# Unused tiles between the operand tiles of TensorE: the places of a fused attention and MoE kernel's tiles in SBUF

## The chip, the core and the metric

The kernel runs on one core of a Trainium2 chip, as one program. The metric is the time of one execution on the device in microseconds, given as the median of three runs. Beside the timed runs there is one profiled execution, and every duration below is read from it.

## What is computed

The first half is a linear attention with a decaying state (4 batches, 8 heads, 768 steps, 48 elements a head); the second half is a dense layer pair with a gate, on 3072 rows of 384:

```python
for t in range(S):
    cur = einsum('bhd,bhe->bhde', u[None] * kt, vt)
    y[:, :, t] = einsum('bhd,bhde->bhe', rt, state + cur)
    state = w[None, :, :, None] * state + einsum('bhd,bhe->bhde', kt, vt)
...
x = y.transpose(0, 2, 1, 3).reshape(B * S, H * D)
h = x @ w_in                # 3072x384 by 384x2048
g = h * cos(h)
out = g @ w_out             # 3072x2048 by 2048x384
```

The MoE weights come in double precision, read as pairs of 32-bit words.

## The kernel before

**The dense part.** Each number of x, w_in, w_out and g is held as a high part and a low part, both of the type fp32r, so that one product takes three matmuls: high by high, high by low, low by high. The rows of x stand in chunks of 128, and three chunks make a block of 384 columns; there are eight blocks. For each block and each of 16 slices of 128 columns of w_in, `mm_h` (L350 to L360) issues nine matmuls: the stationary operand is a 128x128 piece of `w_in_hi` or `w_in_lo`, the moving one is 128x384 of `xh` or `xl` (three runs of 512 bytes in each partition). Its order for one of three parts of the sum is xh with w_in_hi, xl with w_in_hi, xh with w_in_lo. ScalarE and VectorE then turn the result in PSUM into `gh` and `gl` (`whole`, `rest`, `cosine`, and the operations named f_gate, f_gh and f_gl). `mm_o` (L362 to L366) issues three matmuls for each of the three chunks: the stationary operand is a 128x128 piece of gh, gl, gh, and the moving one 128x384 of `w_out_hi`, `w_out_hi`, `w_out_lo`. So there are 8 x 16 x (9 + 9) = 2304 matmuls of 128x384, here called the large ones. Each has a LDWEIGHTS of its own, 128 columns of four bytes, that is 512 bytes in each partition.

**The attention part** is cut into 24 chunks, which TensorE works on between the large matmuls: transposes (L819), scores (L911, L1210), state sums (L978, L1216), outputs (L932, L945, L1283), all in plain fp32 with far smaller shapes. The double-precision weights are read and split (`conv`, L731 to L743) in the first half of the run.

**Order.** A planner in the kernel (`Plan`) gives every operation a cost, a buffer of a ring and a due time, and writes out one order for all engines; a table of due times (`DUES`) sets the order of the first part. It knows nothing of addresses.

**Places in SBUF.** Tiles are laid one behind the other in the order in which the code asks for them. The first 16384 bytes of each partition are the scratch in which GpSimd writes the descriptors of its DMAs (here `dma_start(..., accum_op=ALU.add)`, 27 times). The tiles that the large matmuls read have sizes that are multiples of 512 bytes, and an unused tile of 80 words ahead of them (`const.tile([P, 80], F32, name="gap")`) makes the first of them start at a multiple of 512. So all of them do: w_in_hi, w_in_lo, w_out_hi, w_out_lo, xh, xl, and the rings gh0 to gh2 and gl0 to gl2. Every 128x128 piece of a stationary operand starts 512 bytes, or a multiple of that, behind the start of its tile, and so does every run of a moving one. The last tile ends 352 bytes before the end of the partition's 229376.

Of the kernel before, what the change touches and what calls it, by code (L numbers as in the profile page):

```python
# [9 lines left out]
F32 = mybir.dt.float32  # L10
F32R = mybir.dt.float32r
# [278 lines left out]
def kernel(  # L290
# [11 lines left out]
    nc = tc.nc  # L302
# [5 lines left out]
    P = 128  # L308
# [13 lines left out]
    TB = max(BLOCKS) * C  # L322
# [6 lines left out]
    wts = ctx.enter_context(tc.tile_pool(name="wts", bufs=1))  # L329
# [9 lines left out]
    w_in_hi = wts.tile([P, NK, DFF], F32R, name="w_in_hi")  # L339
    w_in_lo = wts.tile([P, NK, DFF], F32R, name="w_in_lo")  # L340
    w_out_hi = wts.tile([P, NF, DM], F32R, name="w_out_hi")
    w_out_lo = wts.tile([P, NF, DM], F32R, name="w_out_lo")

    w_in_w = moe_w_in.bitcast(I32)
# [35 lines left out]
    with ExitStack() as actx:  # L380
        att = actx.enter_context(tc.tile_pool(name="att", bufs=1))
# [10 lines left out]
        def ring(name, n, shape, dtype):  # L392
            return [Tile(att.tile(shape, dtype, name=f"{name}{i}")) for i in range(n)]
# [9 lines left out]
        R_A = [Tile(A_all[:, n]) for n in range(4)]  # L403
        R_ar = [Tile(A_all[:, n : n + 2], R_A[n : n + 2]) for n in (0, 2)]
        xh = att.tile([P, XS, NK, C], F32R, name="xh")
        xl = att.tile([P, XS, NK, C], F32R, name="xl")
        R_x = [Tile((xh[:, i], xl[:, i])) for i in range(XS)]

        R_f = ring("f", 6, [P, DM], F32)
        R_qi = ring("qi", 1, [P, TB], I32)  # L410
        R_gh = ring("gh", 3, [P, TB], F32R)
        R_gl = ring("gl", 3, [P, TB], F32R)
        R_raw = ring("raw", 2, [P, DM, 2], I32)


# [928 lines left out]
        for i in range(2 * NF):  # L1344
            plan.group = 100 + i
            f, part = divmod(i, 2)
# [18 lines left out]
        for s, (n, f, f0, f1) in enumerate(steps):  # L1365
# [4 lines left out]
            ph, q, qi, gh, gl = Buf(B_H if n >= GRP else B_HX), Buf(R_f), Buf(R_qi), Buf(R_gh), Buf(R_gl)  # L1370
# [128 lines left out]
    with tc.If(ok < 1, label="general"):  # L1499
        with ExitStack() as gctx:  # L1500
            cp = gctx.enter_context(tc.tile_pool(name="cp", bufs=1))
            for i in range(2 * NF):
                f, part = divmod(i, 2)
# [131 lines left out]
```

## Time and profile before

| | |
|---|---|
| median of 3 runs | 489.88 us (489.73 to 490.03) |
| the profiled execution | 489.98 us |
| its span, from the first to the last instruction | 488.3 us |
| outside the span | 1.7 us |
| TensorE, matmuls busy | 481.6 us of the span, 99% |
| TensorE, weight loads busy | 465.6 us, 95% |
| VectorE, ScalarE, GpSimd busy | 379.3, 301.6, 221.1 us |
| granted TensorE clock, mean | 0.997 of 2.4 GHz |

The ends of matmuls in the profile are modelled, and successive matmuls overlap: the 334 ns that the page gives for a large one is the time from its start to its modelled end, not the time that it takes from the next. That is read from the distance between the starts of two matmuls that follow each other.

### The profile page before, as it was taken

What the parts mean: (1) busy time and instruction counts of PE and PEld (TensorE: products, weight loads), DVE (VectorE), ACT (ScalarE), POOL (GpSimd) and SP (SyncE); (2) the same over time, 40 slices, a digit from 0 to 9 for tenths busy, and PEclk for the clock granted to TensorE, in tenths of its full rate; (3) what the DMA queues carried; (4) which work ended last, traced back from release to release, by engine and by line L of the source; (5) the groups of instructions that cost most, each with busy time, mean ns of one, the idle gap of its engine ahead of it and who ended that gap; (6) DMA issues with size and microseconds to landing.
All of it is one profiled execution on the core that took longest, in us unless ns stands there. A gap on an engine that the chain in (4) does not pass through costs nothing.

```text
span 488.3 us, 12920 instructions
## 1 busy us (share of the span) xinstructions
PE 481.6 (99%) x4939; PEld 465.6 (95%) x4939; DVE 379.3 (78%) x790; ACT 301.6 (62%) x718; POOL 221.1 (45%) x227
## 2 busy tenths in 40 slices
PE   8999999999999999999999999999999999999995
PEld 7888999999999999999999999999999999999995
DVE  6988898878999677686896886877867967865552
ACT  5999777767777555556456455465564654644452
POOL 7786225544434856546446245545364275200000
PEclk9999999999999999999999999999999999999998
DMA  8885276865667863766645735655456466100001
GB/s 160 166 191 141 67 221 153 186 155 134 160 156 138 140 121 52 173 104 144 138 97 138 154 92 140 134 158 133 98 128 143 129 148 142 34 30 20 2 0 53
DMA packets 130903, 59.47 MB, mean 122 GB/s; under 512 B 107892, under 2 KB 126740, under 8 KB 130836
## 3 DMA queue, kind: packets, MB, share of 16 engines
q1 hardware_dynamic: 126740, 53.04, 44.2%
q0 software_dynamic: 3888, 5.31, 7.9%
q8 instruction: 40, 0.66, 0.6%
q10 hardware_dynamic: 208, 0.25, 0.1%
q14 instruction: 27, 0.22, 0.1%
HBM read 48.55 MB, written 10.03 MB: 120 GB/s over the span
## 4 chain that ended last, share of the span: by engine, by line
PE 97%; ACT 2%; issue 0%; DVE 0%; DVEq 0%; ACTq 0%
PE bank L366 42%; PE bank L360 41%; PE bank L1210 3%; PE bank L1283 3%; PE bank L819 2%; PE bank L911 2%; PE bank L945 2%; ACT A L884 1%; PE bank L1481 1%; PE bank L932 1%; PE bank L978 1%; ACT kT L861 0%; ACT zt L960 0%; PE bank L583 0%; ACT f L1443 0%
## 5 line engine op out<-in xcount | busy, mean ns | idle before, releaser
L366 PE MATMUL bank<-w_out_hi,gh 128*128 128x384 f32 x384 | 130.9, 341 | 0.0
L360 PE MATMUL bank<-xh,w_in_hi 128*128 128x384 f32 x384 | 129.0, 336 | 0.0
L366 PE MATMUL bank<-w_out_lo,gh 128*128 128x384 f32 x384 | 128.5, 335 | 0.0
L366 PE MATMUL bank<-w_out_hi,gl 128*128 128x384 f32 x384 | 128.4, 334 | 0.0
L360 PE MATMUL bank<-xh,w_in_lo 128*128 128x384 f32 x384 | 128.4, 334 | 0.0
L360 PE MATMUL bank<-xl,w_in_hi 128*128 128x384 f32 x384 | 128.3, 334 | 0.0
L371 ACT ACTIVATE qi<-bank 128x384 int32<-128x384 f32 (+1 forms) x132 | 63.1, 481 | 75.3 <-PE bank L360 74.5
L374 DVE SCALAR_TENSOR_TENSOR f<-bank,qi 128x384 f32<-128x384 f32 (+1 forms) x132 | 70.9, 539 | 31.6 <-ACT qi L371 30.7
L377 ACT ACTIVATE f<-f 128x384 f32<-128x384 f32 (+1 forms) x132 | 67.7, 516 | 44.3 <-DVE f L374 41.5
L1404 DVE TENSOR_TENSOR bank<-bank,f 128x384 f32<-128x384 f32 x126 | 70.7, 561 | 29.1 <-ACT f L377 26.3
L1410 DVE TENSOR_TENSOR gl<-bank,gh 128x384 fp32r<-128x384 f32 x126 | 69.4, 550 | 19.4 <-ACT gh L1407 18.7
L1407 ACT CAST gh<-bank 128x384 fp32r<-128x384 f32 x126 | 60.2, 478 | 38.1 <-DVE bank L1404 35.6
L366 PEld LDWEIGHTS bank<-w_out_hi,gh 128*128 128x128 f32 x384 | 72.0, 188 | 1.7
L360 PEld LDWEIGHTS bank<-xh,w_in_hi 128*128 128x128 f32 x384 | 72.1, 188 | 0.6 <-issue 0.2
L360 PEld LDWEIGHTS bank<-xh,w_in_lo 128*128 128x128 f32 x384 | 72.1, 188 | 0.1
L366 PEld LDWEIGHTS bank<-w_out_hi,gl 128*128 128x128 f32 x384 | 72.1, 188 | 0.0
L360 PEld LDWEIGHTS bank<-xl,w_in_hi 128*128 128x128 f32 x384 | 72.1, 188 | 0.0
L366 PEld LDWEIGHTS bank<-w_out_lo,gh 128*128 128x128 f32 x384 | 72.1, 188 | 0.0
L731 POOL TENSOR_TENSOR f<-f,raw 128x384 int32<-128x384 int32 x32 | 35.2, 1101 | 55.5 <-DVE f L722 24.1
L1152 POOL TENSOR_TENSOR kT<-kT,decT_k 112x512 f32<-112x512 f32 x14 | 18.3, 1310 | 80.1 <-DVE kT L1137 75.1
L1157 POOL TENSOR_TENSOR A<-rT,decT_r 48x512 f32<-48x512 f32 x28 | 36.2, 1292 | 20.7 <-DVE rT L1137 19.6
L1191 POOL TENSOR_TENSOR A<-ident,a 64x512 f32<-64x512 f32 x28 | 30.1, 1074 | 19.7 <-DVE a L1183 18.2
(121 smaller groups left out, 627.8 us busy)
## 6 DMA issues: line engine op xcount, KB each, us to landing
raw<-in_moe_w_in_dram SPq DMA_DIRECT2D x32, 384.0 KB, 3.4
raw<-in_moe_w_out_dram SPq DMA_DIRECT2D x32, 384.0 KB, 3.5
out_dram<-f POOLq DMA_DIRECT2D x27, 192.0 KB, 4.5
out_dram<-f SPq DMA_DIRECT2D x23, 192.0 KB, 2.4
raw<-in_k_dram SPq DMA_DIRECT2D x55, 80.0 KB, 3.1
raw<-in_r_dram SPq DMA_DIRECT2D x55, 80.0 KB, 2.3
k<-in_k_dram SPq DMA_DIRECT2D x28, 96.0 KB, 2.8
f<-in_r_dram SPq DMA_DIRECT2D x28, 96.0 KB, 2.9
```

The lines of the kernel that those rows point to most:

```text
L360: nc.tensor.matmul(ph, a, b_, start=(i == 0), stop=(i == len(mm) - 1))
L366: nc.tensor.matmul(acc, a[:, ts], b_[:, f, :], start=(first and i == 0), stop=(last and i == 2))
L371: nc.scalar.activation(qi, ph, AF.Copy, scale=INV_2PI, bias=0.25)
L374: nc.vector.scalar_tensor_tensor(q, ph, INV_2PI, qi, op0=ALU.mult, op1=ALU.subtract)
L377: nc.scalar.activation(q, q, AF.Sin, scale=TWO_PI, bias=0.5 * math.pi)
L731: return lambda: eng.tensor_tensor(ai(), ai(), cn(), op=ALU.add)
L1152: nc.gpsimd.tensor_tensor(d, d, late_d(decT_k)[0:KP], op=ALU.mult)
L1157: nc.gpsimd.tensor_tensor(by_batch(plane(ar, j))[rows[j]], by_batch(late_t(rT))[rows[j]], late_d(decT_r)[rows[j]], op=ALU.mult)
L1191: nc.gpsimd.tensor_tensor(plane(ar, j)[side[j]], ident2[side[j], None, :].to_broadcast(to), ab()[side[j], :, None].to_broadcast(to), op=AL ...
L1404: nc.vector.tensor_tensor(g()[:, cs], ph()[:, cs], q()[:, cs], op=ALU.mult)
L1407: nc.scalar.copy(gh()[:, cs], g()[:, cs])
L1410: nc.vector.tensor_tensor(gl()[:, cs], g()[:, cs], f32(gh())[:, cs], op=ALU.subtract)
```

## The change

Unused tiles are laid between the operand tiles, so that they no longer all start at the same place within 512 bytes, and the scratch for DMA descriptors is halved to make room:

```diff
     w_out_hi = wts.tile([P, NF, DM], F32R, name="w_out_hi")
+    wts.tile([P, 64], F32, name="gap_w")
     w_out_lo = wts.tile([P, NF, DM], F32R, name="w_out_lo")
...
         xh = att.tile([P, XS, NK, C], F32R, name="xh")
+        att.tile([P, 96], F32, name="gap_x")
         xl = att.tile([P, XS, NK, C], F32R, name="xl")
+        att.tile([P, 96], F32, name="gap_f")
...
-        R_gh = ring("gh", 3, [P, TB], F32R)
-        R_gl = ring("gl", 3, [P, TB], F32R)
+        R_gh, R_gl = [], []
+        for ring_g, name, gaps in ((R_gh, "gh", (64, 16, 48)), (R_gl, "gl", (64, 32, 32))):
+            for i, gap in enumerate(gaps):
+                att.tile([P, gap], F32, name=f"gap_{name}{i}")
+                ring_g.append(Tile(att.tile([P, TB], F32R, name=f"{name}{i}")))
+        att.tile([P, 64], F32, name="gap_r")
...
-    nc = _bacc.Bacc("TRN2", target_bir_lowering=False, num_devices=1)
+    nc = _bacc.Bacc("TRN2", target_bir_lowering=False, num_devices=1, dynamic_dma_scratch_size=8192)
```

A word is four bytes, so the starts of the tiles, as the rest after division by 512, become:

| tile | before | after |
|---|---|---|
| w_in_hi, w_in_lo, w_out_hi | 0 | 0 |
| w_out_lo, and the attention's k, v, r, kT, rT and A tiles behind it | 0 | 256 |
| xh | 0 | 256 |
| xl | 0 | 128 |
| f (six buffers), qi | 0 | 0 |
| gh0, gh1, gh2 | 0, 0, 0 | 256, 320, 0 |
| gl0, gl1, gl2 | 0, 0, 0 | 256, 384, 0 |
| raw (two buffers) and the state tiles behind it | 0 | 256 |

The unused tiles are written and read by nothing. The instructions, their order on each of the five engines and the semaphores that they wait for are the same row for row; only the addresses differ, and the line numbers of the file (a line of before stands 1 further down from L342 on, 2 from L406 on, 3 from L407 on and 7 from L413 on).

While a large matmul streams its moving operand, TensorE loads the stationary operand of the next matmul. There are 2276 places in the program where one large matmul directly follows another. Counted over the program's order, the start of the stationary piece that is loaded, less the start of the moving operand that is being read, modulo 512, is:

| stationary less moving, modulo 512 | 0 | 64 | 256 | 320 | 384 |
|---|---|---|---|---|---|
| places before | 2276 | 0 | 0 | 0 | 0 |
| places after | 372 | 122 | 1140 | 129 | 513 |

The 372 are those in which gh2 or gl2 is loaded while w_out_hi is read (252), and those in which gh0 is loaded while w_out_lo or xh is read (120).

## Rows read from the trace of the kernel before

**Rows 1.** The page's first part: busy time, share of the span, instructions.

```profile
PE 481.6 (99%) x4939; PEld 465.6 (95%) x4939; DVE 379.3 (78%) x790; ACT 301.6 (62%) x718; POOL 221.1 (45%) x227
```

**Rows 2.** The chain that ended last, shares of the span by engine and by line.

```profile
PE 97%; ACT 2%; issue 0%; DVE 0%; DVEq 0%; ACTq 0%
PE bank L366 42%; PE bank L360 41%; PE bank L1210 3%; PE bank L1283 3%; PE bank L819 2%; PE bank L911 2%; PE bank L945 2%; ACT A L884 1%; PE bank L1481 1%; PE bank L932 1%; PE bank L978 1%; ACT kT L861 0%; ACT zt L960 0%; PE bank L583 0%; ACT f L1443 0%
```

**Rows 3.** Waits of TensorE: us in total, times, longest us.

```profile
PE bank L1481 <- DVE pq L474: 1.2, 1, 1.2
PE bank L911 <- ACT kT L861: 0.2, 1, 0.2
```

**Rows 4.** Busy time by stretch: length, then busy (instructions) of each engine.

```profile
core 0: us, PE busy (x) PEld busy (x) DVE busy (x) ACT busy (x) POOL busy (x), PEclk, DMA share, GB/s
58.00:168.00 110.00, 110.00 (x635) 109.78 (x634) 95.91 (x203) 79.39 (x179) 51.80 (x53) 1.00 0.68 158
60.00:80.00 20.00, 20.00 (x118) 20.00 (x117) 18.96 (x45) 15.62 (x38) 5.41 (x6) 1.00 0.59 189
120.00:160.00 40.00, 40.00 (x233) 40.00 (x232) 36.05 (x75) 29.17 (x66) 17.95 (x19) 1.00 0.68 150
```

**Rows 5.** Timeline near 130 us: start, length, engine, line.

```profile
129.90 0.33 PE L360 MATMUL bank<-xh,w_in_hi 128*128 128x384 f32 x1
129.90 0.19 PEld L360 LDWEIGHTS bank<-xl,w_in_hi 128*128 128x128 f32 x1
130.07 0.33 PE L360 MATMUL bank<-xl,w_in_hi 128*128 128x384 f32 x1
130.07 0.19 PEld L360 LDWEIGHTS bank<-xh,w_in_lo 128*128 128x128 f32 x1
130.25 0.33 PE L360 MATMUL bank<-xh,w_in_lo 128*128 128x384 f32 x1
130.25 0.19 PEld L360 LDWEIGHTS bank<-xh,w_in_hi 128*128 128x128 f32 x1
```

**Rows 6.** One line's matmuls, L819: duration min/median/max, first and last start.

```profile
L819 PE MATMUL bank<-ident,vr x40: 272/273/421, 5.7 to 38.3; 128*112 128x128 f32 x40
```

**Rows 7.** Timeline of TensorE's matmuls near 38 us: transposes.

```profile
38.02 0.60 PE L819 MATMUL bank<-ident,vr 128*112 128x128 f32 x4
```

**Rows 8.** Groups of weight loads by shape: count, busy us, mean ns of one.

```profile
L366 PEld LDWEIGHTS bank<-w_out_hi,gl 128*128 128x128 f32 x384 | 72.1, 188 | 0.0
...
L1283 PEld LDWEIGHTS bank<-A,vr 128*32 128x32 f32 x448 | 12.9, 109 | 2.2 <-DVE bank L1404 1.0 <-issue 1.0 <-DVE gl L1410 0.2
```

**Rows 9.** Timeline of TensorE's matmuls at 217 us, after a stretch of small ones.

```profile
217.22 0.44 PE L366 MATMUL bank<-w_out_hi,gh 128*128 128x384 f32 x1
217.50 0.33 PE L366 MATMUL bank<-w_out_hi,gl 128*128 128x384 f32 x1
217.66 0.34 PE L366 MATMUL bank<-w_out_lo,gh 128*128 128x384 f32 x1
217.84 0.35 PE L360 MATMUL bank<-xh,w_in_hi 128*128 128x384 f32 x1
218.03 0.34 PE L360 MATMUL bank<-xl,w_in_hi 128*128 128x384 f32 x1
```

**Rows 10.** Timeline of TensorE's matmuls at 170 us, the second and the eighth large one.

```profile
170.36 0.34 PE L366 MATMUL bank<-w_out_hi,gl 128*128 128x384 f32 x1
...
171.43 0.33 PE L360 MATMUL bank<-xl,w_in_hi 128*128 128x384 f32 x1
```

**Rows 11.** Timeline of TensorE's matmuls near 47 us: scores, then large ones.

```profile
47.13 0.39 PE L911 MATMUL bank<-rT,kT 48*128 48x128 f32 x4
```

**Rows 12.** One line's matmuls, L911: duration min/median/max, first and last start.

```profile
L911 PE MATMUL bank<-rT,kT x160: 272/272/373, 8.6 to 47.2; 48*128 48x128 f32 x160
```

**Rows 13.** The page's groups on other engines that touch the moved tiles.

```profile
L1410 DVE TENSOR_TENSOR gl<-bank,gh 128x384 fp32r<-128x384 f32 x126 | 69.4, 550 | 19.4 <-ACT gh L1407 18.7
L1407 ACT CAST gh<-bank 128x384 fp32r<-128x384 f32 x126 | 60.2, 478 | 38.1 <-DVE bank L1404 35.6
L731 POOL TENSOR_TENSOR f<-f,raw 128x384 int32<-128x384 int32 x32 | 35.2, 1101 | 55.5 <-DVE f L722 24.1
```

**Rows 14.** Waits over all engines, the longest of ScalarE for TensorE.

```profile
ACT qi L371 <- PE bank L360: 74.5, 83, 3.1
```

**Rows 15.** GpSimd's DMAs: the line's issues and the time to landing.

```profile
L1455 POOL DMA_DIRECT2D out_dram<-f x27: 862/1012/1522, 80.3 to 209.7; - x27
...
DMA to landing us min/median/max: 3.6/4.5/6.3
```

## Prediction

> **What bounds the kernel now.** I read the busy times first, then the chain of work that ended last, the stretches, and last the starts of single matmuls. TensorE is busy for 481.6 of 488.3 us [rows 1] and holds 97% of the chain, 83 points of it in the two lines of the large matmuls [rows 2]. It waited for other engines for 1.4 us in the whole run [rows 3], so what one large matmul takes from the next is what the kernel takes.
>
> That distance is read from a stretch in which nothing but large matmuls runs, 58 to 168 us: 110 us hold 635 of them, 173.2 ns each [rows 4]. The single starts say the same (129.90, 130.07, 130.25), and show the next weight load starting with each matmul, not after it [rows 5]. The clock granted there is 1.00 of 2.4 GHz [rows 4], at which 384 columns, one a cycle, are 160 ns. What does a stream of matmuls with a load each cost on top? The transposes tell: four of 128 columns span 0.60 us with a last one of 0.272 [rows 6, 7], so they follow each other by (0.60 - 0.272)/3 = 109 ns, which is 2 cycles a column (106.7 ns) and 2.5 ns. By that a large matmul would take 160 + 2.5 = 162.5 ns. It takes 10.8 more. Over the 2276 places where one follows another this is 2276 x 10.8 ns = 24.6 us: the stake of this change, 5% of the run.
>
> Where do the 10.8 ns come from? Loading is not too slow by itself: a load of 128 columns is recorded with 188 ns, one of 32 with 109 [rows 8], so a column is 79/96 = 0.82 ns and 128 columns are 105 ns, well under 173. But the two streams do disturb each other. After a stretch of small matmuls the distances are not 173 at once: at 217 us they run 0.16, 0.18, 0.19 [rows 9], and at 170 us six of them take 171.43 - 170.36 = 1.07 us, 178 ns each [rows 10]. The same instructions on the same kind of tiles take anything from about 168 to 185 ns, until they settle at 173. Only the moment at which the load starts within the matmul differs.
>
> **The change part by part.** No instruction is added, removed or moved, so all of the cost is in durations.
>
> *The distance of the loaded piece from the streamed operand.* At all 2276 places it is 0 modulo 512 before; after, it is something else at 2276 - 372 = 1904. The trace of before holds no large matmul at another distance, so the price is bounded from both sides by the nearest rows. If the 10.8 ns are a collision of the two reads that only equal places bring, all of it goes: 1904 x 10.8 = 20.6 us. If the new distance acts as another phase does, the shortest distance seen (0.16, taken as 168 ns [rows 9]) gives 1904 x 5 = 9.5 us back, and the mean of an unsettled row (178 ns [rows 10]) costs 1904 x 5 = 9.5 us; the longest seen (0.19, about 185 ns) would be 1904 x 12 = 23 us lost. The value I take is 0, for three reasons. First, the tiles before differ in all places above 512 bytes (pieces of w_in, w_out, g and three runs of x at ever new addresses), and 173 holds over all of them in the long stretch [rows 4]: nothing in this trace goes by place. Second, equal places alone do no harm: the scores read kT and rT, both at 0 modulo 512, and four of them span 0.39 us [rows 11] with 0.272 for the last [rows 12], so the second pair starts 0.12 us after the first at most, about the 109 ns of the transposes, whose two operands lie at different places (ident at 160). Both have a column every two cycles. What the large ones have that these have not is a full-rate stream, one column a cycle: a shared rate of reading, which would not care for addresses, fits this as well as a collision. Third, a phase of a nanosecond or two already changes the distance [rows 9, 10], and 64 to 384 bytes are many columns; if the two streams settle by themselves after any disturbance, they may settle at the same 173 from any start.
>
> The Trainium skill speaks against an effect too: its page "TensorE: Matmul & The Clock Gate", section "Step-by-step: what each phase is for", gives TensorE two independent read ports to SBUF, one for the moving operand and one for weight loads, so that loading the next weights takes nothing from the running matmul. By it the change is worth 0. The trace agrees only in part: the same page's section "Back-to-back issue gap" has N/2.4 + 2.5 ns, 162.5 for 384, and the 173.2 ns [rows 4] are not that. So what the page rules out is happening in some form, and no run of before shows in which.
>
> *The writers.* ScalarE writes gh, VectorE reads it and writes gl, GpSimd reads f and raw: 478, 550 and 1101 ns each [rows 13]. All new starts are multiples of 64 bytes and each operation still runs over the same contiguous words, so I take 0. These lie behind TensorE: ScalarE alone waits 74.5 us for it [rows 14]. If each of the 126 gl were 5% slower, that is 3.5 us spread over the run, inside VectorE's idle time of 488 - 379 = 109 us [rows 1]. Without that cover, at the fullest stretch (18.96 of 20 us busy, 60 to 80 us [rows 4]), 5% would be 1 us on the path.
>
> *Half the scratch for GpSimd's descriptors.* It serves 27 DMAs, all issued between 80.3 and 209.7 us, one in 4.8 us on average, each landed within 6.3 us [rows 15]. So about one is open at a time, and a ring of half the size has to hold no more than that. If one waits for room, GpSimd's later work (the sums of `conv`, the decays) waits behind it; GpSimd is busy for 17.95 of 40 us there [rows 4]. I take 0, with at most one landing, 6.3 us, which would have to stand in a place without cover.
>
> *Sum:* 489.98 us of the profiled execution (span 488.3 and 1.7 around it), less 0. The median of the three runs is 489.88, 0.1 below it; I give 489.8.
>
> **The rivals.**
>
> *Equal places collide, and the collision goes.* For it: the 10.8 ns are there, and phase matters. Against it: the scores. It gives 489.98 - 20.6 = 469.4. Part could be lost in new waits: TensorE needs results 6% sooner, and in the fullest stretch VectorE's 18.96 us stand against 20.0 - 1904/2276 x 20.0 x 10.8/173.2 = 18.96. VectorE would just hold there and all later stretches are emptier (36.05 of 40). With 1 us for it, 470.4.
>
> *Another phase, a part of it:* the streams settle nearer to the shortest distance seen: 489.98 - 9.5 = 480.5, and anything between that and no change.
>
> *The other side: the streams settle worse.* Today they lock at 173 after each disturbance; at new distances, of which there are five, changing from matmul to matmul, they may never settle, and keep the 178 ns seen at 170 us [rows 10]. That gives 489.98 + 9.5 = 499.5. It decides against the change as soon as the mean over the 1904 places is above 173.7, since 1904 x 0.5 ns is 1 us.
>
> *The room for descriptors binds:* GpSimd's DMA issues, now 0.86 to 1.52 us long [rows 15], become several us long; at most 6.3 us, 496, and more likely hidden. I count it in the slower cases.
>
> **How the numbers follow.** A measurement of this kernel tells changes from about 0.2%, 1 us, on (three runs lie within 0.3 us). No change: 0.33, the likeliest single case, at 489.8, with 489.0 to 490.7 as its own range. The collision goes: 0.24. A part of it: 0.19. Slower, by unsettled streams (0.21) or by descriptors (0.03): 0.24. So faster 0.24 + 0.19 = 0.43, same 0.33, slower 0.24. Cases of both signs hold most of the chance, so the range reaches to both: from 469, the foot of the full gain, to 499, the unsettled price, which leaves out a gain at more places than the 1904, and streams that run worse than 178 ns, together under 0.2.
>
> **What would show it.** In the stretch 58 to 168 us the count of large matmuls: 635 again if places don't matter; 1904/2276 of 10.8 ns less, 164.3 on average, would put 670 there; 178 would put 618. By kind: if equal places collide, the large matmuls before a load of gh2 or gl2 keep 173 and those before gh1 or gl1 fall to 162.5, within one run; if all three buffers show the same distance, place is not the cause. The groups of the other engines [rows 13] should stay within 2% of 550, 478 and 1101 ns; if gl or gh move by more, the writers were mis-sized. L1455 should keep a median near 1.0 us; several us would show the smaller scratch. The prediction is wrong if the distance of large matmuls is not 173 in that stretch, in either direction, and right for the wrong reason if distances change by kind and cancel.

## The result, and the profile after

The changed kernel takes 493.14 us, median of 3 runs (492.95 to 493.7), against 489.88: ratio 1.0069, 95% interval 1.0046 to 1.0092. It became slower by 3.3 us, where no change was forecast; the time still lies inside the stated range of 469 to 499 us. Its profiled execution also took 493.14 us, with a span of 491.3 us.

The page's first part and the chain that ended last, after:

```profile
PE 484.6 (99%) x4939; PEld 468.8 (95%) x4939; DVE 381.0 (78%) x790; ACT 301.8 (61%) x718; POOL 221.2 (45%) x227
...
PE 97%; ACT 2%; issue 0%; DVE 0%; DVEq 0%; ACTq 0%
```

TensorE is busy for 3.0 us more than in [rows 1] with the same 4939 instructions, and holds the same 97% of the chain as in [rows 2]. Its waits for other engines are those of [rows 3] to the tenth of a microsecond:

```profile
PE bank L1488 <- DVE pq L481: 1.2, 1, 1.2
PE bank L918 <- ACT kT L868: 0.2, 1, 0.2
```

So the time did not go into a new wait. The stretch that [rows 4] begin with, after:

```profile
58.00:168.00 110.00, 110.00 (x631) 110.00 (x631) 95.75 (x202) 79.11 (x179) 50.99 (x52) 1.00 0.67 157
```

Four large matmuls fewer stand in the same 110 us, at the same granted clock of 1.00: 174.3 ns each, where it was 173.2. Which ones became longer is seen in the groups of TensorE's lines (count, busy us, mean ns of one). Two groups after:

```profile
L361 PE MATMUL bank<-xl,w_in_hi 128*128 128x384 f32 x384 | 130.7, 340 | 0.0
...
L361 PE MATMUL bank<-xh,w_in_lo 128*128 128x384 f32 x384 | 128.7, 335 | 0.0
```

and the first of them before:

```profile
L360 PE MATMUL bank<-xl,w_in_hi 128*128 128x384 f32 x384 | 128.3, 334 | 0.0
```

The matmul that reads xl grew by 6 ns, from start to modelled end. While it runs, the piece of w_in_lo for the next matmul is loaded, and this is the largest kind of place whose distance became 384. The one behind it, which reads xh, is at 335.

To price it, I took the starts of all 2304 large matmuls from both traces, and added up by kind what each takes until the next starts, at the 2276 places where one directly follows another:

| what is read, while what is loaded | places | distance after, modulo 512 | mean before, ns | mean after, ns | change in all, us |
|---|---|---|---|---|---|
| xl while w_in_lo | 384 | 384 | 173.4 | 179.0 | +2.15 |
| w_out_hi while gl1 | 129 | 384 | 179.4 | 181.6 | +0.29 |
| w_out_lo while gh1 | 84 | 64 | 174.0 | 176.3 | +0.20 |
| xh while gh1 | 38 | 64 | 173.7 | 172.6 | -0.04 |
| w_out_hi while gh1 | 129 | 320 | 173.7 | 173.3 | -0.05 |
| xh while w_in_hi | 645 | 256 | 174.6 | 175.1 | +0.28 |
| all others | 867 | 0 or 256 | | | +0.21 |

(The means hold the first matmul behind each of the 28 stretches of small ones, 283 ns on average; these fall mostly on the places where gl is loaded. Without them, the places where gl1 is loaded go from 173.4 to 175.8 ns.) The rows add up to 3.03 us. The rest of the span stayed: the first large matmul starts at 39.04 us before and 39.03 after, the stretches of small matmuls between the large ones take 45.44 and 45.40 us in all, and the tail behind the last large start 5.59 and 5.68. So 3.03 of the 3.08 us by which the span grew lie in these distances, and seven tenths of them at the 384 places of xl.

The other engines, after:

```profile
L1417 DVE TENSOR_TENSOR gl<-bank,gh 128x384 fp32r<-128x384 f32 x126 | 69.4, 551 | 19.6 <-ACT gh L1414 19.2
L1414 ACT CAST gh<-bank 128x384 fp32r<-128x384 f32 x126 | 60.3, 478 | 36.7 <-DVE bank L1411 35.7
...
L738 POOL TENSOR_TENSOR f<-f,raw 128x384 int32<-128x384 int32 x32 | 35.2, 1102 | 55.7 <-DVE f L729 22.9
```

They stand at 551, 478 and 1102 ns, within 1 ns of [rows 13]. GpSimd's DMA line, after, is as in [rows 15], with a median landing of 4.9 us for 4.5:

```profile
L1462 POOL DMA_DIRECT2D out_dram<-f x27: 859/1012/1517, 80.5 to 210.8; - x27
```

### The profile page after: what moved, and what is told of

It is laid out like the page before. It is cut to its first block, busy times and chain, and to the rows that moved or that the text cites. A ratio compares the mean times of both kernels' runs of the same rounds, so it can differ in the third digit from the quotient of the medians.

```text
span 491.3 us, 12920 instructions
## 1 busy us (share of the span) xinstructions
PE 484.6 (99%) x4939; PEld 468.8 (95%) x4939; DVE 381.0 (78%) x790; ACT 301.8 (61%) x718; POOL 221.2 (45%) x227
## 4 chain that ended last, share of the span: by engine, by line
PE 97%; ACT 2%; issue 0%; DVE 0%; DVEq 0%; ACTq 0%
PE bank L367 42%; PE bank L361 41%; PE bank L1217 3%; PE bank L1290 3%; PE bank L826 2%; PE bank L918 2%; PE bank L952 2%; ACT A L891 1%; PE bank L1488 1%; PE bank L939 1%; PE bank L985 1%; ACT kT L868 0%; ACT zt L967 0%; PE bank L590 0%; ACT f L1450 0%
## 5 line engine op out<-in xcount | busy, mean ns | idle before, releaser
L361 PE MATMUL bank<-xl,w_in_hi 128*128 128x384 f32 x384 | 130.7, 340 | 0.0
L738 POOL TENSOR_TENSOR f<-f,raw 128x384 int32<-128x384 int32 x32 | 35.2, 1102 | 55.7 <-DVE f L729 22.9
```

The source lines that it names most:

```text
L361: nc.tensor.matmul(ph, a, b_, start=(i == 0), stop=(i == len(mm) - 1))
L738: return lambda: eng.tensor_tensor(ai(), ai(), cn(), op=ALU.add)
```

## The experiments

After this comparison, theory A was: a large matmul's time depends on the distance between the piece that is loaded and the operand that is read, and the costly places are those whose distance is no multiple of 256, the 384 of xl first. The rivals were the other parts of the change: the absolute places of the tiles, the smaller scratch, the places of the loads and of the other engines' tiles. All kernels below have the scratch of 8192 bytes, as the change has. Where a ratio is given it is to the kernel before, timed on the same chip, with a 95% interval. The kernels p1 to p3, q1 and q2 ran once each, so they have no interval. Means by kind are read from the starts, as in the table above; where a text below says that every kind stands at some value, the first matmul behind a stretch of small ones and single stops of over 200 ns are left out.

**xl moved from 128 to 256, the rest of the change kept** (e1, against the change):

```diff
-        att.tile([P, 96], F32, name="gap_x")
         xl = att.tile([P, XS, NK, C], F32R, name="xl")
-        att.tile([P, 96], F32, name="gap_f")
+        att.tile([P, 64], F32, name="gap_f")
...
```

> The change, but xl starts at 256 like xh instead of 128; f, g and raw stay where the change puts them. Theory A: most of the 3.3 us of the change is lost at the 384 places where w_in_lo is loaded while xl streams (179 ns after the change, 173.4 before), because xl lies 128 bytes off a multiple of 256: this run then shows 173 to 174 ns there and takes about 3.3 - 2.1 = 1.2 us more than before, 491.1. Theory B: every distance other than 0 disturbs the streams a little, wherever it is: the xl places stay at or above 176 ns and the time stays near 493.

492.29 us against 490.18: ratio 1.0034, 1.0022 to 1.0047 (the two medians alone give 1.0043). The group of xl is back at its old length:

```profile
L361 PE MATMUL bank<-xl,w_in_hi 128*128 128x384 f32 x384 | 128.4, 334 | 0.0
```

The places of xl are at 174.1 ns on average. What is left of the loss, 0.34% or 1.7 us by the ratio and 2.1 by the medians, is more than the 1.2 that A expected of the places of gh1 and gl1. The distances from large one to large one add up to 2.7 us more than before in this trace; 0.9 of that are single stops, distances of 0.2 to 0.4 us between 97 and 108 us, which hold 1.0 us above 174 ns each here, 0.13 in before and nothing in the change. Their cause is shown with e7 below.

**xl alone at 128, all else as before** (e2, against before):

```diff
+        att.tile([P, 32], F32, name="gap_x")
         xl = att.tile([P, XS, NK, C], F32R, name="xl")
+        att.tile([P, 96], F32, name="gap_f")
```

> Before, with xl alone moved to 128 (and the scratch of 8192 bytes, as in the change). Theory A: the xl places go to 179 ns as in the change, 384 x 5.6 ns = 2.1 us, so 492.0. Theory B: with all other places at distance 0 the loss at xl is at most its share of the places, 384 of 1904, of the 3.3 us: 0.7 us, 490.6.

492.76 us against 490.18: 1.0053, 1.0032 to 1.0075. The same two views as above, of this run:

```profile
58.00:168.00 110.00, 110.00 (x631) 109.72 (x630) 95.58 (x203) 79.03 (x179) 50.69 (x52) 1.00 0.67 158
```

```profile
L360 PE MATMUL bank<-xl,w_in_hi 128*128 128x384 f32 x384 | 130.8, 341 | 0.0
```

One tile moved by 128 bytes brings back 631 matmuls in the stretch, 341 ns for the group and 179.0 ns for the distance: most of the loss of the change. The time is 0.8 us above what theory A gave.

**The smaller scratch alone** (e3):

```diff
-    nc = _bacc.Bacc("TRN2", target_bir_lowering=False, num_devices=1)
+    nc = _bacc.Bacc("TRN2", target_bir_lowering=False, num_devices=1, dynamic_dma_scratch_size=8192)
```

> Before, with the scratch of 8192 bytes alone; all starts modulo 512 as before. Both theories: 489.9, within 0.3 us, and 173.3 ns for the large matmuls. If it takes 491 or more, the smaller scratch (or the place in SBUF in steps of 8192 bytes) carries a part of the change's loss.

490.52 us against 490.18: 1.0011, 0.9995 to 1.0027. The large matmuls are at 173 to 174 ns at every kind of place. The scratch costs nothing that can be measured.

**All tiles moved by 128, all distances 0 as before** (e4, against before):

```diff
-    const.tile([P, 80], F32, name="gap")
+    const.tile([P, 112], F32, name="gap")
```

> Before with the scratch of 8192 bytes and everything shifted by 128 bytes, so that all operands of the large matmuls start at 128 modulo 512 and the distance between loaded and streamed operand is 0 at all 2276 places. If the distance counts: 173.3 ns and 489.9 us. If the place of the streamed operand itself counts (128 off a multiple of 256 is bad): 179 ns at all places, 2276 x 5.6 = 12.7 us more, 502 or so; for loads that start at 128 too, possibly more.

492.93 us against 490.18: 1.0054, 1.0033 to 1.0076. Slower, but not in the large matmuls: the sum of their distances is 398.5 us, for 398.2 before. So absolute places don't count for them, and the expected 489.9 us was missed for another reason: the loss is in the start. TensorE's timeline of this run, and of before, around the first large matmul:

```profile
39.80 0.65 PE L819 MATMUL bank<-ident,k 128*112 128x128 f32 x4 [0.41 <-POOL k L839]
...
41.31 0.45 PE L360 MATMUL bank<-xh,w_in_hi 128*128 128x384 f32 x1
```

```profile
39.04 0.44 PE L360 MATMUL bank<-xh,w_in_hi 128*128 128x384 f32 x1
```

The first large one starts 2.3 us later, behind small ones that waited for k. By lines, the chain that ended last now goes over the loads of k and vr, which is the entry to look for in it (in [rows 2] no DMA stands there):

```profile
PE bank L366 42%; PE bank L360 41%; PE bank L1210 3%; PE bank L1283 3%; DMA k<-in_k_dram 2%; DMA vr<-in_r_dram 1%; POOL f L834 1%; PE bank L911 1%; POOL k L839 1%; POOL f L868 1%; PE bank L819 1%; PE bank L945 1%; PE bank L932 0%; SPq L798 0%; PE bank L978 0%
```

**Only k, v, r and the tiles of the attention behind them at 128** (e6, against before):

```diff
+        att.tile([P, 32], F32, name="gap_k")
         R_k = ring("k", 3, [P, H, DP], F32)
...
+        att.tile([P, 96], F32, name="gap_xh")
         xh = att.tile([P, XS, NK, C], F32R, name="xh")
```

> Before with the attention's k, v, r, kT, rT and A tiles alone at 128, everything of the dense part at 0. In the run with all tiles at 128 the large matmuls took what they take before, but the first of them started at 41.3 us instead of 39.0. If that comes from where the rows of k, v and r land: the first large matmul again starts at 41 us, and the time is 2 to 2.7 us above before, 492 to 492.6. If not: 489.9 to 490.5.

492.77 us against 490.83: 1.0045, 1.0026 to 1.0063. The large matmuls take 398.3 us in all, and the first starts at 41.42 us: the whole loss of e4 again. In the first 39 us, the DMA view of before, of e4 and of e6 (packets, MB, the packets' time as a share of 16 engines; then issues, KB each, median us to landing):

```profile
q1 hardware_dynamic: 30656, 6.79, 83.0%
...
k<-in_k_dram SPq DMA_DIRECT2D x10, 192.0 KB, 3.5
```

```profile
q1 hardware_dynamic: 29575, 6.28, 107.9%
...
k<-in_k_dram SPq DMA_DIRECT2D x10, 192.0 KB, 4.9
```

```profile
q1 hardware_dynamic: 29131, 6.19, 105.8%
...
k<-in_k_dram SPq DMA_DIRECT2D x10, 192.0 KB, 4.8
```

A packet takes 0.830 x 16 x 39 us / 30656 = 16.9 ns before, 22.8 in e4 and 22.7 in e6. These are mostly rows of 48 words, 192 bytes, that land in slots of 256 bytes. The packets of 192 bytes alone take 15.6 ns on average before, 22.0 in e4 and 21.8 in e6. From 128 on, each row starts off a multiple of 256 and crosses one; the runs don't tell these two apart. GpSimd's operation on k (L839) takes 1.02 us before and as long in e4 and e6, so it is the loads that are late and not the work on them. The change puts these tiles at 256, where rows start at a multiple of 256: its packets of 192 bytes take 15.6 ns, and its start is as before (39.03 us). So this is a second effect of places, which the change doesn't touch.

The Trainium skill has a rule that fits this: its page "DMA: Bandwidth & Descriptors", section "How a descriptor splits into AXI transactions", lets a transaction start only at a multiple of 256 bytes, and counts what is fetched below a descriptor's start as lost. It speaks of reads; the rows here differ in where they are written, so the runs show an effect in the same direction on the other side of the transfer.

**One constant distance of -128 everywhere** (e5: w_out_hi, w_out_lo, xh and xl at 128, w_in and g at 0, against before). It was made to tell apart two readings of the 179 ns: V, that the value of the distance sets the time at each place, and J, that only a change of the distance from one matmul to the next costs.

```diff
+    wts.tile([P, 32], F32, name="gap_h")
     w_out_hi = wts.tile([P, NF, DM], F32R, name="w_out_hi")
...
+        att.tile([P, 96], F32, name="gap_k")
         R_k = ring("k", 3, [P, H, DP], F32)
...
+        att.tile([P, 32], F32, name="gap_xh")
         xh = att.tile([P, XS, NK, C], F32R, name="xh")
...
+        att.tile([P, 96], F32, name="gap_f")
         R_f = ring("f", 6, [P, DM], F32)
```

> All streamed operands of the large matmuls (xh, xl, w_out_hi, w_out_lo) at 128 and all loaded pieces (w_in, gh, gl) at 0, so the distance is -128 at all 2276 places, as it was at the xl places of the change that took 179 ns; k, v, r and raw stay at 0. Theory V, the value of the distance counts: 179 ns at all places, 2276 x 5.6 = 12.7 us more, 502.6. Theory J, only a change of the distance from one large matmul to the next counts: 173.3 to 173.8 ns and the time of before within 0.5 us, since the distance never changes.

495.38 us against 490.83: 1.0088, 1.0058 to 1.0119. The stretch, and the three groups of the first product:

```profile
58.00:168.00 110.00, 110.00 (x628) 109.89 (x627) 95.20 (x202) 78.46 (x177) 50.39 (x52) 1.00 0.67 156
```

```profile
L361 PE MATMUL bank<-xh,w_in_hi 128*128 128x384 f32 x384 | 130.4, 340 | 0.0
L361 PE MATMUL bank<-xl,w_in_hi 128*128 128x384 f32 x384 | 129.8, 338 | 0.0
...
L361 PE MATMUL bank<-xh,w_in_lo 128*128 128x384 f32 x384 | 129.7, 338 | 0.0
```

Neither reading holds. Every kind is at 175 to 176 ns (128 no longer costs 179 where it is constant), and the distances between starts don't settle at one value: in long stretches they repeat, as 174, 174, 175, 181, 176 ns near 130 us, and most groups of five in a row add up to 879 or 880 ns. So a constant distance of -128 costs too, with no step in it. Over 2276 places that is 5.0 us, the most of all.

**Other distances.** p1 to p3 set xh and xl to 64, 32 and 192 and the three buffers of g to three values each (a constant distance within a product of x, changing ones in that of g); q1 and q2 set xl alone to 32 and 96 (e2's gaps with other lengths). In short, p1 and q1 against before:

```diff
+        att.tile([P, 16], F32, name="gap_xh")
         xh = att.tile([P, XS, NK, C], F32R, name="xh")
...
+        att.tile([P, 112], F32, name="gap_f")
         R_f = ring("f", 6, [P, DM], F32)
...
+        for ring_g, name, gaps in ((R_gh, "gh", (8, 104, 8)), (R_gl, "gl", (16, 104, 8))):
...
```

```diff
+        att.tile([P, 8], F32, name="gap_x")
         xl = att.tile([P, XS, NK, C], F32R, name="xl")
+        att.tile([P, 120], F32, name="gap_f")
```

> One look, read by the distances of the large matmuls and not by the whole time: xh and xl at 64 (loaded less streamed = -64 in the first product), gh and gl at 32, -64 and -32 in their three buffers (w_out at 0). The change itself showed 173 to 174 ns at distances 0 and 256, 176 at 64 and 179 at -128. Theory C: the distance counts modulo 256 and 0 is the best place: nothing here lies clearly under 173.3 ns, and -64 costs 3 ns or more. Theory D: the two reads collide at 0 already, and a small distance takes them apart: at 32, -32 or -64 some places fall towards 162.5 ns.

> One look: xh and xl at 32 (distance -32), gh and gl at 64, 96 and 128. Theory C: 64 shows about 176, 128 about 179 ns or what -128 showed, 96 between; nothing under 173. Theory D: one of 64, 96, 128 or -32 falls well under 173.

> One look: xh and xl at 192 (distance -192, which is 64 modulo 256), gh and gl at 160, 192 and 224 (which are -96, -64, -32 modulo 256). Theory C, with the distance counting modulo 256: -192 shows what 64 showed in the change, 176 ns, and 192 and 224 show what -64 and -32 show in the first of these three runs. If the two differ by more than 2 ns, it is not modulo 256.

> One look: before with xl alone at 32, so the distance steps by -32 and back within each group of three. Theory J, by what single steps from a settled stretch showed so far (174 ns at -32, 180 at +32): the mean over the three lies above 173.3, by 1 to 3 ns. Theory V: whatever the places at -32 alone cost, 172 to 173 ns, so no loss, or a gain of 1 ns at a third of the places.

> One look: before with xl alone at 96, steps of -96 and back. Single steps of -96 (160 modulo 256) showed 172 to 173 ns and of +96 177, so by theory J the mean of the three is again at or above 173.3; a mean clearly under it would be a way to a faster kernel, which neither theory expects.

| run | time, us | before on the same chip | mean at xl, ns | sum of the large distances, us |
|---|---|---|---|---|
| p1 | 492.78 | 491.18 | 174.0 | 400.5 |
| p2 | 492.33 | 491.18 | 173.5 | 401.4 |
| p3 | 493.67 | 491.18 | 174.3 | 401.5 |
| q1 | 492.12 | 490.83 | 172.8 | 400.7 |
| q2 | 495.34 | 490.83 | 176.1 | 403.8 |

(Before: 398.2. The sum of p3 holds 1.8 us, that of p2 1.1, of single stops near 91 to 114 us.) None is better than before, and no kind of place comes near 162.5 ns. Within the product of x, a constant distance of -32, -64 or -192 stands at 173 to 174 ns, as 0 does; theory C had expected 176 or more for -64 and -192, and there it was wrong. Where xl differs from xh by 32 or 96, what one kind gains another loses: in q1 the 384 places of xl give back 0.23 us, and the 645 where w_in_hi is loaded while xh is read cost 1.66. The mean over the product of x, without first matmuls and stops, is 174.9 ns in q1 and 176.2 in q2, above 173.3 as theory J expected.

What a change of the distance costs is seen at single steps. Taken are, from all these runs, the change, e1, e2 and e7, the places at which three matmuls stood at one distance with 173 or 174 ns each, and the distance then changed. Left out are places with a small matmul or a stop among the three matmuls before or the three behind. The first matmul at the new distance, and four together from the step on, took on average:

| step, modulo 256 | cases | first, ns | four together, ns |
|---|---|---|---|
| 0 (steps of 256) | 279 | 173.3 | 693.3 |
| 32 | 65 | 179.6 | 708.0 |
| 64 | 76 | 176.6 | 705.6 |
| 96 | 22 | 177.4 | 701.6 |
| 128 | 134 | 180.7 | 701.0 |
| 160 | 160 | 174.6 | 702.1 |
| 192 | 62 | 174.1 | 694.8 |
| 224 | 177 | 173.3 | 699.1 |

A step of 256 is free. For 160 and 224 the longer matmuls come behind the first one.

**All starts at multiples of 256** (e7: the change with xl, gh1 and gl1 at 256 for 128, 320 and 384, against the change):

```diff
-        att.tile([P, 96], F32, name="gap_x")
         xl = att.tile([P, XS, NK, C], F32R, name="xl")
-        att.tile([P, 96], F32, name="gap_f")
+        att.tile([P, 64], F32, name="gap_f")
...
-        for ring_g, name, gaps in ((R_gh, "gh", (64, 16, 48)), (R_gl, "gl", (64, 32, 32))):
+        for ring_g, name, gaps in ((R_gh, "gh", (64, 0, 64)), (R_gl, "gl", (64, 0, 64))):
...
```

> The change with the three odd places made even: xl, gh1 and gl1 at 256 modulo 512 (128, 320 and 384 in the change), and the rest of it as it is, so that every distance of the 2276 places is 0 or 256 modulo 512. If distances count modulo 256 alone (theory A), every kind of large matmul is at 173 to 174 ns after the next, 634 to 636 large ones stand in 58 to 168 us, and the time is within 0.1% of before: 489.9 to 490.7 where before has 490.2. If the change of the distance modulo 512 costs too (rival: a step of 256 also disturbs), the places where 256 and 0 follow each other, xh to w_out and between gh1 and gh2, are above 175 ns, and it stays at 491.0 or more. If something else of the change costs (the place of f, raw, or the weights' rows), the large matmuls are at 173 and the start or the stretches of small ones are longer than before by more than 0.5 us.

490.53 us against 490.38 (12 and 17 runs): 1.0002, 0.9991 to 1.0014. The group of xl and the stretch:

```profile
L361 PE MATMUL bank<-xl,w_in_hi 128*128 128x384 f32 x384 | 128.4, 334 | 0.0
```

```profile
58.00:168.00 110.00, 109.89 (x633) 109.33 (x632) 95.53 (x202) 79.36 (x179) 51.27 (x52) 1.00 0.67 157
```

Every kind of place is back at 173 to 174 ns, although 1782 of the 2276 distances are 256 and they change from matmul to matmul. The 633 instead of 635 are two single stops, which hold 0.57 us of this trace. The rows of e7's weight loads tell what ended them:

```profile
L361 PEld LDWEIGHTS bank<-xh,w_in_hi 128*128 128x128 f32 x384 | 72.1, 188 | 0.9 <-DVE gl L1417 0.4
L361 PEld LDWEIGHTS bank<-xh,w_in_lo 128*128 128x128 f32 x384 | 72.1, 188 | 0.2 <-DVE w_in_lo L741 0.2
```

In both stops TensorE waited for VectorE: once for the operation that writes gl, and once for the one that writes w_in_lo when the weights are split. The stops of e1, p2 and p3 have such waits too, for VectorE or ScalarE. They are waits for other engines, and not longer reads.

So the whole loss of the change, to within the 0.14% of the interval, is in the three tiles that don't stand at a multiple of 256. How it splits among them is less sure: xl alone costs 0.53% (e2), gh1 and gl1 alone 0.34% (e1, with some 1 us of stops in its trace), all three 0.69%.

## Why the prediction was wrong

**What bounds the kernel** was right. Each nanosecond of a large matmul is on the path: the span grew by 3.08 us and the distances by 3.03.

**The distance term is the step that failed**: "The value I take is 0". Measured, it is 3.03 us. Of the three reasons for 0, the first ("nothing in this trace goes by place") could not be seen in that trace: all operands of the large matmuls shared their place modulo 256 there, and this, as e7 shows, is what counts. The second, that equal places alone do no harm, is borne out: giving up equal places brings nothing at any distance tried. The third, "they may settle at the same 173 from any start", is the one that e5 refutes: at a constant -128 they don't settle at 173, but repeat distances of 174 to 181 with a mean near 176. The reading behind it, that a phase of a nanosecond or two changes the distance, isn't borne out by the trace of before either: the load is recorded as starting 2 to 4 ns after the matmul beside it in the unsettled rows (168 to 185 ns), and 2 to 3 ns after it in the settled ones.

**The Trainium skill's rule** that was weighed there, two independent read ports in "TensorE: Matmul & The Clock Gate", section "Step-by-step: what each phase is for", gives 0 for this change. The 179.0 ns at the places of xl in e2, where xl alone was moved, are against it: what is loaded, and where it lies, does reach the running matmul in this kernel.

**The rival that came true** is "the streams settle worse". Its price per disturbed place was near: 178 ns from [rows 10], 5 ns above 173, and 5.6 ns were measured at xl; whether the two have the same cause isn't shown. The count was not, and the forecast gave this rival a chance of 0.21. It took all 1904 places at which the distance is no longer 0 modulo 512; but 1140 of these have 256, which e7 shows to be free. Modulo 256 there are 251 places at 64 and 513 at 128, 764 in all, and 764 x 5 ns = 3.8 us would have given 493.8. The 380 beside xl cost less than 5 ns, 0.4 us in all in the table, and some of the cost falls on their neighbours. The rival's condition, a mean above 173.7 over the 1904 places, was met: they hold 2.89 of the 3.03 us, 1.5 ns each on top.

**The collision that goes** and **a part of it** are refuted for every distance tried: by the prediction's own sign, the places before a load of gh1 and gl1 should have fallen to 162.5 ns, and where w_out_hi is read they stand at 173.3 and, without the first ones behind small matmuls, 175.8. No kernel of the study has a smaller sum of distances than before. Where the 10.8 ns above 162.5 come from stays open, and so does why a constant distance of 128 modulo 256, or a step of the distance, makes the matmuls longer; the runs show which places cost, not the mechanism.

**The writers and the scratch** were right at 0: within 1 ns [rows 13], and 1.0011 with 1 in the interval for e3. **The sum** around them needed no other term: the start, the small stretches and the tail are the same within 0.1 us.

## What to carry to other kernels

Where TensorE loads a stationary piece for each matmul while another streams, keep the loaded and the streamed tiles at the same place modulo 256 bytes; here equal places are the best of those tried, and one tile 128 bytes off costs 0.5%. A trace in which all tiles share a place can't tell whether place matters: a price of 0 from it is a guess, and the count of places in it depends on the modulus, which only a run with another distance shows. After a move of tiles, read the distances by kind (what is read while what is loaded); the average of a stretch shows a loss, and the kind shows its place.

## What the runs showed of the hardware beside this

Rows of 192 bytes that land in SBUF at 128 modulo 256 take 21.8 ns a packet for 15.6, and where loads bound the start this costs 0.45% of the run (e6). The same program, laid elsewhere, also has single stops of TensorE between 91 and 114 us, 0.1 us in all before, 0.6 in e7, 1.8 in p3. They are waits for VectorE and ScalarE in the stretch in which the weights are split; why they differ from trace to trace was not tried.
